# Placing the second layer's accumulations among the first layer's, and the last pairs' normalisation, in a fused attention and MLP kernel

## The chip, the cores and the metric

The kernel runs on one core of one Trainium2 chip. The metric is the device time of one execution in microseconds (us); lower is better. The engines are called TensorE (PE in the profile, its weight loads PEld), VectorE (DVE), ScalarE (ACT), GpSimd (POOL) and SyncE (SP, which here only issues transfers).

## What is computed

`x` has 2048 tokens of 640 features. It is normalised once, and the result feeds a multi-head attention with 32 heads of 20 features and a two-layer MLP (640 to 1536 to 640, GELU between) that normalises its input again. Both results are added to `x`.

```python
B, S, D, H = 1, 2048, 640, 32          # F = 1536
xn = _layernorm(x)
# attention
q, k, v = split(xn @ wqkv)             # (B, H, S, 20) each
p = softmax(einsum("bhqd,bhkd->bhqk", q, k) * 20 ** -0.5)
a = einsum("bhqk,bhkd->bhqd", p, v).reshape(B, S, D) @ wo
# MLP
h = gelu(_layernorm(xn) @ w1 + b1)
m = h @ w2 + b2
return x + a + m
```

## The kernel before

After a first part (to about 220 us) that normalises, projects q, k and v and splits the weights into pairs of 16-bit numbers, one loop (L1143) runs over 256 *groups*. The heads are taken in pairs: `ORDER` (L39) runs over pairs 0 to 11 with both halves of the queries each, then over pairs 12 to 15 with the first half of the queries, then over pairs 12 to 15 with the second half. Each such entry has eight groups: two blocks of 512 queries by four times four blocks of 128 keys.

A group issues, in this order:

- two blocks of scores (`scores`, L705: two matmuls `s` each, then ScalarE's exponential into `p`), a `tick()`, `rest` for the first block, and one portion of *fill* (`other`, L1129);
- two more blocks of scores, a `tick()`, `rest` for the others, and the products of the previous group's probabilities with v (`pv`, L730, matmuls `o`).

`rest` (L720) has VectorE compute `low`, the 16-bit remainder of two of the four probability blocks; the products need it one group later. After every fourth group `pv` has ScalarE copy its result out of PSUM (`ev`), and after eight `unload` (L771) stores it with six transfers on SP's queue.

The fill is TensorE's other work, cut into *units* by the generator `mlp` (L1015) and, after it, `projection` (L1064). `other` spreads a unit over two to four groups, so that each group gets about the same amount. The MLP goes through eight chunks of 256 tokens:

- `layer1(mc, f)` (L966) makes two of the twelve blocks of hidden features of a chunk: 30 matmuls `pu` into the one PSUM bank of pool `psM`. At its end `gelu` (L910) begins, seven operations of VectorE and one tanh of ScalarE, spread over the following ticks; the first of them (`u`, L914) sets the bank free. The result goes to `hT`, of which there are two buffers.
- `layer2(mc, j, hf)` (L998) makes 128 tokens by 320 output features from `hT`: 36 matmuls `py` into the same bank. At its end `addup` (L940) adds it onto `xb` (one operation of VectorE, L942), which sets the bank free. `xb` has one buffer: after every second such unit it is stored (L947), loaded anew with `x` (L995), and `b2` is added by a transfer on GpSimd's queue (L996).

A chunk has six first-layer units and, of the chunk before it, four second-layer units; `mlp` says in which order they stand. When a chunk's last first-layer unit is issued, the features of the chunk after the next are loaded; after the last chunk's, the output weights `wo` are loaded into the place of `w1`, and `prep_late` (L671) splits them on VectorE, eight ticks later.

The attention's results are *normalised* by their sums in `finish` (L824), for two or three pairs of heads and half of the queries at a time: sums are loaded (`lt`, L835), inverted and stored (L876 to L885), and then, for 512 queries at a time, two partial results (`oa`, L867) and the inverses (`rb`, L897) are loaded, added, multiplied and split into 16-bit numbers (L900, L902, L904, L906), and stored to `oscr` (L907). These generators are moved on by `tick` (L652), one step a tick. There are two lists: those in `sides` take a step at every tick; those in `patient` only at ticks where nothing else has just given VectorE work, or in steps that are marked as waiting. The finishes stand in one queue (`fins`) and run one after the other in one generator, `finishing`, which begins in `patient`. `unload` puts it over to `sides` under a condition (L786).

When all units of `mlp` are issued, `projection` follows: 256 tokens at a time (a *piece*), 15 matmuls `z` for each 128 tokens by 320 features, added onto the MLP's result by L1047. It needs all finishes of its half of the queries and the split of `wo`; `ahead` (L1054) loads the first piece (L1041, L1042) as soon as the first half's finishes are done. What is left of it after the last group runs at the end by itself, from about 1274 us.

Of the kernel before, what the change touches and what calls it, by code (L numbers as in the profile page):

```python
# [27 lines left out]
NPAIR = H // 2  # L28
# [9 lines left out]
TAIL = 12  # L38
# [6 lines left out]
def mha_mlp_kernel(tc, x, wqkv, wo, w1, b1, w2, b2, out):  # L45
# [4 lines left out]
    with (  # L50
# [580 lines left out]
        with ExitStack() as scope:  # L631
# [8 lines left out]
            sides, patient = [], []  # L640
# [89 lines left out]
            def pv(units):  # L730
# [29 lines left out]
                if last:  # L760
                    if cc == 0:
                        evs[g, hf] = m1.tile([P, 2, 512], F32, tag="ev", name="ev")
                    nc.scalar.activation(evs[g, hf][:, cc], pv.o, AF.Copy)  # L763
                    if cc == 1:
                        unload(g, hf, evs.pop((g, hf)))

            def dma(g, hf):

                return (nc.scalar if (g, hf) == ORDER[-1] else nc.sync).dma_start

            def unload(g, hf, ev):  # L771
                cols = slice(hf * 1024, (hf + 1) * 1024)
                direct.extend([ev] if (g, hf) == ORDER[-1] else [])
                for p in range(0 if direct else 2):
                    dma(g, hf)(lpart[p, hf, 2 * g : 2 * g + 2, :].rearrange("a (c t) -> a c t", c=2),
                                      ev[PAD + DH + VW * p :: 64])
                    for a in range(2):
                        q0, r = 64 * a + PAD + VW * p, (2 * g + a) * DH
                        dma(g, hf)(opart[p, r : r + DH, cols].rearrange("d (c t) -> d c t", c=2),
                                          ev[q0 : q0 + DH])  # L780
                if g + 1 in ENDS:
                    fins.append(finish(g + 1 - UNITS[ENDS.index(g + 1)], g + 1, hf))
                    if len(fins) == 1:
                        patient.append(finishing())
                        runner[:] = patient[-1:]
                    if hf == 1 and g + 1 > TAIL and runner[0] not in sides:  # L786

                        patient.remove(runner[0])
                        sides.append(runner[0])
# [6 lines left out]
            fins, direct, runner = [], [], []  # L796
# [22 lines left out]
            def finishing():  # L819
                while fins:  # L820
                    yield from fins[0]
                    fins.pop(0)
# [133 lines left out]
            def load_chunk(mc):  # L956
                t0 = mc * MC
                xnt = early.pop(0) if early else load_features(mc)
                r2f = m1.tile([P, MC], F32, tag="r2f", name="r2f", bufs=2)
                nc.sync.dma_start(r2f, rscr[None, t0 : t0 + MC].to_broadcast([P, MC]))  # L960
                xs[mc] = xnt, r2f
                unscaled.append(r2f)
                if mc > 1:
                    patient.append(scale_ahead(r2f))

            def layer1(mc, f):  # L966
                xnt, r2f = xs[mc]
                if f == 0:
                    hTs[mc] = m0.tile([P, KF, 2, MC], F16, tag="hT", name="hT")
                ps = psM.tile([P, 2, MC], F32, tag="m", name="pu")  # L970
                for i in range(2):
                    n = 0
                    fo_ = (f + i) % 4 * P
                    for k in range(KD):
                        for a, b in PASS:
                            nc.tensor.matmul(ps[:, i], w1v[:, k, (f + i) // 4, a, fo_ : fo_ + P], xnt[:, k, b, :],  # L976
                                             start=(n == 0), stop=(n == 3 * KD - 1))
                            n += 1
                            if n % 3 == 0:
                                if i == 1 and n == 15:  # L980
                                    begin(gelu(ps, r2f, hTs[mc], f))
                                yield 0.3276
                if f == KF - 2:
                    if mc + 2 < NMC:
                        load_chunk(mc + 2)
                    if mc + 1 == NMC:
                        sides.append(ahead())
                        sides.append(prep_late(wot, wov, wo.rearrange("(k p) n -> p k n", p=P), KD, 8))
# [9 lines left out]
            def layer2(mc, j, hf):  # L998
                t0 = mc * MC + j * P
                if t0 == 0 and hf == 0:  # L1000
                    load_xb(0)
                ps = psM.tile([P, 512], F32, tag="m", name="py")
                n = 0
                for f in range(KF):
                    for a, b in PASS:
                        nc.tensor.matmul(ps[:, :320], hTs[mc][:, f, a, j * P : (j + 1) * P],  # L1006
                                         w2v[:, f, b, hf * 320 : (hf + 1) * 320],
                                         start=(n == 0), stop=(n == 3 * KF - 1))
                        n += 1
                        if n % 2 == 0:  # L1010
                            if n == 36:
                                begin(addup(ps, xbs[t0], t0, hf))
                            yield 0.272

            def mlp():  # L1015
                load_chunk(0)
                load_chunk(1)
                yield 0.0
                for mc in range(NMC + 1):
                    first = [layer1(mc, f) for f in range(0, KF, 2)] if mc < NMC else []  # L1020
                    second = [layer2(mc - 1, j, hf) for j in range(MC // P) for hf in range(2)] if mc else []
                    done[0] = mc == NMC
                    for i in range(6):
                        if i < len(first):
                            yield 2 * KD, 3.276
                            yield from first[i]
                        if 0 < i <= len(second):
                            yield 3 * KF // 2, 4.896
                            yield from second[i - 1]

            pieces = {}

# [81 lines left out]
            def chain():  # L1114
                yield from mlp()
                yield from projection()
# [167 lines left out]
```

## Time and profile before

| | |
|---|---|
| time, median of 3 runs | 1341.68 us (1340.11 to 1343.48) |
| the profiled execution | 1341.9 us, of it 1340.0 us from the first to the last instruction |
| granted TensorE clock, mean | 0.999 |
| exponentials (L713, ScalarE) | 1024, busy 972.8 us |
| `low` (L725, VectorE) | 512, busy 614.5 us |
| `o` (L742), `s` (L711), TensorE | share of the chain of waits 28% and 18% |
| `py` (L1006), `pu` (L976), TensorE | 1152 matmuls, busy 178.5 us; 1440, busy 178.2 us |

A row of the trace in order of time begins with its start and its length in us, then engine, line, operation, `out<-in` by the program's names, shapes, and how many instructions were merged into it (x4). In square brackets is how long the engine had been idle before it and which instruction ended that. In a row of stretches, each engine's busy time is followed by its number of instructions. On the page, the line of an engine gives busy time, share of the span and number of instructions; the chain of waits is the chain that ended last, followed back from the last instruction. A line of transfers gives their size and, where it is known, the median time from issue to landing.

### The profile page before, as it was taken

The numbers are of one execution on the slowest core, as the hardware profiler recorded it, in microseconds if no ns is written. First come the engines' busy times: TensorE is split into PE (matmuls) and PEld (weight loads), VectorE is DVE, ScalarE is ACT, GpSimd is POOL, SyncE is SP. The second block draws the span as 40 slices with busy tenths as digits, with TensorE's granted clock in tenths as the row PEclk, the third lists the DMA queues.
The fourth block names the chain that finished last, engine by engine and source line by source line (L and its number), as shares of the span: only waits on it lengthen the run. The fifth ranks groups of instructions, "written<-read, shape, count | busy, mean of one in ns | idle before, by whom it ended". The sixth has DMA issues, their size and how long they took to land.

```text
span 1340.0 us, 29065 instructions
## 1 busy us (share of the span) xinstructions
PE 1328.6 (99%) x11647; PEld 588.6 (44%) x11647; DVE 1055.9 (79%) x1436; ACT 1130.1 (84%) x1306; POOL 37.5 (3%) x85
## 2 busy tenths in 40 slices
PE   9999999999999999999999999999999999999998
PEld 6645546443344433434433344334333444333366
DVE  7766945998779887978897878888887988888732
ACT  7754525999999999999999999999999999999900
POOL 3010000000000000000000000000000000000000
PEclk9999999999999999999999999999999999999999
DMA  9768731111112232122322032313032323334366
GB/s 279 253 197 183 125 128 58 34 53 43 49 52 78 87 83 73 44 69 67 91 76 71 19 103 56 88 56 94 19 83 78 85 64 103 90 113 121 104 208 187
DMA packets 100150, 129.54 MB, mean 97 GB/s; under 512 B 24276, under 2 KB 66328, under 8 KB 100012
## 3 DMA queue, kind: packets, MB, share of 16 engines
q1 hardware_dynamic: 96652, 120.25, 31.5%
q0 software_dynamic: 2912, 6.90, 2.8%
q8 instruction: 92, 1.51, 0.5%
q10 hardware_dynamic: 448, 0.51, 0.1%
q14 instruction: 46, 0.38, 0.1%
HBM read 82.14 MB, written 42.51 MB: 93 GB/s over the span
## 4 chain that ended last, share of the span: by engine, by line
PE 86%; DVE 6%; ACT 4%; issue 2%; DMA 1%; SPq 0%; ACTq 0%; DVEq 0%; POOL 0%; POOLq 0%
PE o L742 28%; PE s L711 18%; PE py L1006 13%; PE pu L976 10%; PE qkp L325 7%; PE z L1089 4%; PE vp L398 3%; DVE low L725 2%; ACT p L713 1%; PE warm L222 1%; ACT wv L431 1%; DMA oa<-opart 0%; DVE u L914 0%; ACT qkhl L340 0%; DVE u L916 0%
## 5 line engine op out<-in xcount | busy, mean ns | idle before, releaser
L713 ACT ACTIVATE p<-s 128x1024 f32<-128x1024 f32 x1024 | 972.8, 1045 | 35.0 <-PE s L711 28.6
L725 DVE TENSOR_TENSOR low<-p 128x1024 f16<-128x1024 f32 x512 | 614.5, 1219 | 144.9 <-ACT p L713 144.2
L742 PE MATMUL o<-p,vfull 128*32 128x512 bf16 (+1 forms) x4096 | 430.0, 493 | 0.0
L711 PE MATMUL s<-qs,ks 61*128 61x512 f16 x2048 | 311.9, 381 | 1.1 <-ACT p L713 1.1
L711 PEld LDWEIGHTS <-ks 61*128 61x128 f16 x2048 | 61.1, 94 | 280.1 <-issue 279.1
L1006 PE MATMUL py<-w2t,hT 128*128 128x320 f16 x1152 | 178.5, 300 | 0.5 <-DVE u L914 0.3
L976 PE MATMUL pu<-xm,w1t 128*128 128x256 f16 x1440 | 178.2, 273 | 0.0
L976 PEld LDWEIGHTS <-w1t 128*128 128x128 f16 x1440 | 131.0, 98 | 64.6 <-issue 51.0
L1006 PEld LDWEIGHTS <-hT 128*128 128x128 f16 x1152 | 102.5, 98 | 88.5 <-issue 54.1
L325 PE MATMUL qkp<-xnt,wv 128*128 128x512 f16 x600 | 131.1, 379 | 1.4 <-DVE vfull L410 0.9
L742 PEld LDWEIGHTS <-vfull 128*32 128x32 f16 x3072 | 59.8, 95 | 139.2 <-issue 108.5
L742 PE MATMUL o<-low,vfull 128*32 128x512 f16 x1024 | 102.9, 378 | 0.4 <-DVE low L725 0.2
L325 PEld LDWEIGHTS <-wv 128*128 128x128 f16 x600 | 58.1, 98 | 71.4 <-DVE vfull L410 1.2
L742 PEld LDWEIGHTS o<-p,vfull 128*32 128x32 f32 x2048 | 62.5, 108 | 52.6
L1089 PE MATMUL z<-w1t,ot 128*128 128x320 f16 x480 | 69.0, 304 | 0.4 <-DVE acc L1047 0.4
L340 ACT ACTIVATE qkhl<-qkp,qks 128x1024 f16<-128x1024 f32 (+1 forms) x24 | 23.2, 967 | 54.6 <-PE qkp L325 33.0
L398 PE MATMUL vp<-wv,xnt 128*128 128x320 f16 x480 | 66.7, 299 | 0.0
L1089 PEld LDWEIGHTS <-ot 128*128 128x128 f16 x480 | 46.7, 99 | 24.3 <-issue 5.9
L398 PEld LDWEIGHTS <-xnt 128*128 128x128 f16 x480 | 46.7, 98 | 18.4
L341 DVE SCALAR_TENSOR_TENSOR qkhl<-qkp,qks,qkhl 128x1024 f16<-128x1024 f32 (+1 forms) x24 | 26.5, 1105 | 32.6 <-ACT qkhl L340 32.5
L1047 DVE SCALAR_TENSOR_TENSOR acc<-z,sc,acc 128x320 f32<-128x320 f32 x32 | 17.4, 546 | 40.7 <-PE z L1089 40.5
L763 ACT ACTIVATE ev<-o 128x512 f32<-128x512 f32 x64 | 39.3, 614 | 2.7 <-PE o L742 2.7
(190 smaller groups left out, 672.4 us busy)
## 6 DMA issues: line engine op xcount, KB each, us to landing
qkscr<-qkhl SPq DMA_DIRECT2D x40, 256.0 KB
opart<-ev SPq DMA_DIRECT2D x124, 80.0 KB
ks<-qkscr SPq DMA_DIRECT2D x120, 80.0 KB
qs<-qkscr SPq DMA_DIRECT2D x192, 40.0 KB
oa<-opart SPq DMA_DIRECT2D x32, 240.0 KB
xt<-in_A_x_dram SPq DMA_DIRECT2D x16, 320.0 KB
xscr<-xnt SPq DMA_DIRECT2D x4, 1280.0 KB
xm<-xscr SPq DMA_DIRECT2D x8, 640.0 KB
```

What stands on the lines that cost most here:

```text
L325: nc.tensor.matmul(ps[:, i, :], wv[:, k, q, a, mm * P : (mm + 1) * P], xnts[c][:, k, b, :], start=(k + n == 0), stop=(k == KD - 1 and n == 2))
L340: nc.scalar.activation(hl[:, 0, i0:i1], ps[:, i0:i1], AF.Copy, scale=a)
L341: nc.vector.scalar_tensor_tensor(hl[:, 1, i0:i1], ps[:, i0:i1], a, hl[:, 0, i0:i1], ALU.mult, ALU.subtract)
L398: nc.tensor.matmul(ps[:, hf, :320], xnts[c][:, k, a, j * P : (j + 1) * P], wv[:, k, 2, b, hf * 320 : (hf + 1) * 320], start=(n == 0), stop ...
L711: nc.tensor.matmul(ps[:, a, :], ks[64 * a : 64 * a + 61, kb * P : (kb + 1) * P], qs[64 * a : 64 * a + 61, cc * 512 : (cc + 1) * 512], star ...
L713: nc.scalar.activation(pt, ps, AF.Exp, scale=QS)
L725: nc.vector.tensor_sub(low, pt, upper(pt))
L742: nc.tensor.matmul(pv.o[32 * q : 32 * q + 32, :], src[:, v0 - PAD * (1 - q % 2) :][:, :32], t, start=q not in pv.begun, stop=last, skip_gr ...
L763: nc.scalar.activation(evs[g, hf][:, cc], pv.o, AF.Copy)
L976: nc.tensor.matmul(ps[:, i], w1v[:, k, (f + i) // 4, a, fo_ : fo_ + P], xnt[:, k, b, :], start=(n == 0), stop=(n == 3 * KD - 1))
L1006: nc.tensor.matmul(ps[:, :320], hTs[mc][:, f, a, j * P : (j + 1) * P], w2v[:, f, b, hf * 320 : (hf + 1) * 320], start=(n == 0), stop=(n == ...
L1089: nc.tensor.matmul(ps[:, :320], ot[:, k, a, j * P : (j + 1) * P], wov[:, k, b, h * 320 : (h + 1) * 320], start=(n == 0), stop=(n == 3 * KD ...
```

## The change

In `unload`, the finishing generator is put over to `sides` not only when pairs 13 and 15 with the second half of the queries are unloaded, but also at pair 15 with the first half.

In `mlp`, the four second-layer units of a chunk no longer follow the second, third, fourth and fifth first-layer unit, but the second, third, fifth and sixth. With 0 to 5 for the first-layer units and a to d for the second-layer units of the chunk before, the order was 0 1 a 2 b 3 c 4 d 5 and is 0 1 a 2 b 3 4 c 5 d.

```diff
@@ unload
-                    if hf == 1 and g + 1 > TAIL and runner[0] not in sides:
+                    if (hf == 1 or g + 1 == NPAIR) and g + 1 > TAIL and runner[0] not in sides:
 
                         patient.remove(runner[0])
                         sides.append(runner[0])
@@ mlp
                     for i in range(6):
                         if i < len(first):
                             yield 2 * KD, 3.276
                             yield from first[i]
-                        if 0 < i <= len(second):
+                        if second and i % 3:
+
                             yield 3 * KF // 2, 4.896
-                            yield from second[i - 1]
+                            yield from second.pop(0)
```

Nothing else differs. The amount of work, the number of transfers and the sizes of all tiles are the same. After the edit in `mlp` the lines of the changed kernel are one higher.

## The prediction

> **What bounds the kernel now.** I read the engines' busy times and the chain of waits on the page first, then busy time by stretches, then TensorE's rows in order of time.
>
> ```profile
> PE 1328.6 (99%) x11647; PEld 588.6 (44%) x11647; DVE 1055.9 (79%) x1436; ACT 1130.1 (84%) x1306; POOL 37.5 (3%) x85
> PE 86%; DVE 6%; ACT 4%; issue 2%; DMA 1%; SPq 0%; ACTq 0%; DVEq 0%; POOL 0%; POOLq 0%
> 240.00:1240.00 1000.00, 998.20 (x9338) 400.53 (x9335) 852.09 (x1018) 965.87 (x1081) 13.59 (x16) 1.00 0.26 72
> 1273.70:1340.00 66.30, 59.97 (x445) 42.90 (x441) 21.14 (x41) 0.60 (x1) 0.00 (x0) 0.97 0.64 197
> ```
>
> The last two rows are stretches: length, then busy PE, PEld, DVE, ACT, POOL, clock. The change touches the first one, the attention loop. TensorE is called busy for 998 of 1000 us there, ScalarE 966, VectorE 852. Since a busy PE may hide stops, I take instead how long one turn of the loop (a "group") lasts, from the start of its run of feed-forward matmuls to the start of the next:
>
> ```profile
> 603.07 1.16 PE L976 MATMUL pu<-xm,w1t 128*128 128x256 f16 x9
> 606.89 1.48 PE L976 MATMUL pu<-xm,w1t 128*128 128x256 f16 x12
> 611.02 1.26 PE L1006 MATMUL py<-w2t,hT 128*128 128x320 f16 x8
> ...
> 619.11 1.26 PE L1006 MATMUL py<-w2t,hT 128*128 128x320 f16 x8
> ...
> 627.20 1.81 PE L976 MATMUL pu<-xm,w1t 128*128 128x256 f16 x15
> ...
> 631.66 1.81 PE L976 MATMUL pu<-xm,w1t 128*128 128x256 f16 x15
> ```
>
> A group with 9 pu lasts 3.82, with 12 pu 4.13, with 15 pu 4.46, an 8 and a 10 py together 8.09. The length follows the matmuls put in, so TensorE sets the pace, and what can be won is only what a group lasts beyond this. A chunk is 31 groups: three first-layer units as 15+15, three as 9+9+12, four second-layer units as 8+10+8+10. That is 6×4.46 + 6×3.82 + 3×4.13 + 8×8.09 = 126.8 us. The same place in seven chunks (the second group of a chunk's first second-layer unit):
>
> ```profile
> 306.79 1.53 PE L1006 MATMUL py<-w2t,hT 128*128 128x320 f16 x10
> 434.82 1.53 PE L1006 MATMUL py<-w2t,hT 128*128 128x320 f16 x10
> 561.79 1.53 PE L1006 MATMUL py<-w2t,hT 128*128 128x320 f16 x10
> 689.80 1.53 PE L1006 MATMUL py<-w2t,hT 128*128 128x320 f16 x10
> 817.20 1.53 PE L1006 MATMUL py<-w2t,hT 128*128 128x320 f16 x10
> 944.53 1.53 PE L1006 MATMUL py<-w2t,hT 128*128 128x320 f16 x10
> 1072.02 1.53 PE L1006 MATMUL py<-w2t,hT 128*128 128x320 f16 x10
> ```
>
> The cycles last 128.03, 126.97, 128.01, 127.40, 127.33 and 127.49. The second shows what a cycle can be; over it the others lose 1.06 + 1.04 + 0.43 + 0.36 + 0.52 = 3.41 us. The whole kernel holds little more than that to win.
>
> **What the first edit removes.** Now the first-layer units five, zero and one of neighbouring chunks stand next to each other. VectorE's work for such a row of three:
>
> ```profile
> 671.83 0.68 DVE L914 TENSOR_TENSOR u<-pu,r2f 128x512 f32<-128x512 f32 x1
> ...
> 673.89 1.22 DVE L725 TENSOR_TENSOR low<-p 128x1024 f16<-128x1024 f32 x1
> 675.02 0.68 DVE L920 SCALAR_TENSOR_TENSOR w<-w,u 128x512 f32<-128x512 f32 x1
> 675.63 1.22 DVE L725 TENSOR_TENSOR low<-p 128x1024 f16<-128x1024 f32 x1
> 676.76 0.68 DVE L900 TENSOR_TENSOR oa<-oa 120x512 f32<-120x512 f32 x1
> 677.36 1.22 DVE L725 TENSOR_TENSOR low<-p 128x1024 f16<-128x1024 f32 x1
> 678.50 0.69 DVE L924 SCALAR_TENSOR_TENSOR u<-w,u 128x512 f32<-128x512 f32 x1
> ...
> 680.41 1.22 DVE L725 TENSOR_TENSOR low<-p 128x1024 f16<-128x1024 f32 x1
> 680.68 1.48 PE L976 MATMUL pu<-xm,w1t 128*128 128x256 f16 x12
> ...
> 685.49 1.25 PE L1006 MATMUL py<-w2t,hT 128*128 128x320 f16 x8 [0.28 <-DVE u L914]
> ```
>
> Start to start, a low costs 1.13, the GELU's first three operations 2.06, its L920 0.61, its last three 1.91 (4.58 in all), and each operation of a normalisation 0.60 (its cast less). A group needs two lows, 2.27. I add up, group by group in the built order, VectorE's load less the group's length. In the groups of 9, 12, 8 from 676.9 the sum goes 1.35, 2.14, 3.27 us, and TensorE stops: 685.49 − 680.68 = 4.81 against 4.13, then 689.80 − 685.49 = 4.31 against 3.91, together 1.08. In the other cycles the sum reaches 3.27, 1.35, 2.43, 1.35 and 2.55, and they lose as listed; below 2 a stop is hardly to be seen, above 2.2 there is one.
>
> In the built order of the changed kernel units five and zero have a second-layer unit between them, with 16.2 us of TensorE and 0.5 of VectorE beyond the lows. Pairs are left: zero and one, three and four. The same sum gives, outside the first chunk (which has the old order in both), at most 2.50, 2.44 and 2.32 at three places (near 433, 495 and 1002 us) and 1.84 elsewhere.
>
> Not all of the 3.41 goes, because some stops are ScalarE's:
>
> ```profile
> 421.90 1.16 PE L976 MATMUL pu<-xm,w1t 128*128 128x256 f16 x9
> ...
> 423.67 0.39 PE L711 MATMUL s<-qs,ks 61*128 61x512 f16 x2 [0.29 <-ACT p L713]
> ...
> 426.17 1.48 PE L976 MATMUL pu<-xm,w1t 128*128 128x256 f16 x12
> ...
> 933.99 0.39 PE L711 MATMUL s<-qs,ks 61*128 61x512 f16 x2 [0.25 <-ACT p L713]
> ```
>
> Here a tanh and an unloading copy fall into one 9-group: 426.17 − 421.90 = 4.27, 0.45 too long; I take 0.41 for the other, scaled by the waits. In the new order both still fall so. Removed: 3.41 − 0.86 = 2.55 (between 2.0 and 3.41). Added: of the three places the first already waits for ScalarE, which lowers its sum by 0.45; the others I put at 0.3 each, 0.6 in all (0 to 1.3, by the 0.52 of the cycle that reached 2.55).
>
> **What both edits move near the end.** The normalisation of the last pairs, first half of the queries, is no longer held back: its second half moves from groups 240–242 to 235–237, with two oa loads, four rb loads and one store on SP's queue; projection piece 0's three loads follow it. The output weights' split moves with unit five from groups 236–243 to 232–239, its load equally far ahead. There VectorE's sum reaches 1.8 in groups of 12, against 1.36 before: nothing added (0 to 0.5).
>
> ```profile
> 1202.10 0.36 SPq L947 DMA_DIRECT2D accscr<-xb  x1
> 1207.69 0.85 POOL L996 DMA_DIRECT2D xb<-in_B_b_dram  x1 [39.32 <-DMA xb<-in_A_x_dram]
> xb<-in_B_b_dram POOLq DMA_DIRECT2D x16, 320.0 KB, 4.4
> 1223.51 1.14 SPq L835 DMA_DIRECT2D lt<-lpart  x2
> 1230.82 0.22 DVE L876 TENSOR_TENSOR lt<-lt 64x64 f32<-64x64 f32 x1 [2.87 <-DMA lt<-lpart]
> ```
>
> One transfer gets a new neighbour: the store L947 of the last-but-one add-up now stands behind piece 0's loads on SP. From L947 to the reloaded xb it takes 1207.69 − 1202.10 + 4.4 = 10.0 us, and the next add-up comes two pairs of 8 and 10 later, 16.2. A load issued right behind piece 0's took 7.3 (1223.51 to 1230.82); by this the 6.2 of cover shrinks to about zero. Behind a late add-up stand the next lows; but the 2.87 us that VectorE waited for lt lengthened no group. I take 0 (0 to 1).
>
> The following normalisation (pairs 12 and 13, second half of the queries) begins about one group earlier, since nothing is before it. Now it does this:
>
> ```profile
> 1247.65 1.40 PE L1089 MATMUL z<-w1t,ot 128*128 128x320 f16 x9
> ...
> 1255.33 1.40 PE L1089 MATMUL z<-w1t,ot 128*128 128x320 f16 x9
> 1256.32 0.69 DVE L900 TENSOR_TENSOR oa<-oa 80x512 f32<-80x512 f32 x1 [2.44 <-DMA oa<-opart]
> ...
> 1264.01 1.40 PE L1089 MATMUL z<-w1t,ot 128*128 128x320 f16 x9
> ```
>
> A 9-and-6 pair of z took 8.68 where the one before took 7.68: 1.00 lost to oa. Its loads stood behind six stores and three loads on SP; in the new order they stand ahead of them. I take the whole 1.00 (0 to 1.00). The last 66.3 us keep their order: nothing.
>
> **Sum.** −2.55 + 0.6 − 1.00 = −2.95 on the profiled execution's 1341.9 us; the median of the runs is 0.2 lower, so 1341.68 − 2.95 = 1338.7, put at 1338.8. With the bounds, the sum lies between −4.4 and +0.8.
>
> **The rivals.** *A, every stop goes:* with less on VectorE its L920, and so the tanh behind it, comes earlier and ScalarE's two stops go as well; the remaining 0.1 to 0.2 of each cycle over 126.8 does too: 3.41 + 1.00 + about 0.6, so 1336.7. For it: the stops come in the same groups as VectorE's sums; against it: ScalarE shows no wait for VectorE there.
>
> *B, pairs overfill VectorE as three did (slower):* seven pairs of units three and four and the split of the output weights, each now with half a normalisation in or behind it, each stopping TensorE as the 680–690 us place did: 8 × 1.08 = 8.6, less 4.4 won, 1345.9. It decides from a sum of about 1.8 on. Against it: the cycle of 126.97 has the same five-to-zero pair and a sum of 1.35.
>
> *C, ScalarE is the bound and nothing is won:* its exponentials, 966 of 1000 us busy, are untouched; stops move and stay, 1341.7. Against it: group lengths follow the matmuls. The Trainium skill (Perfetto Trace Analysis, Identifying the Most-Contended Engine) calls matmul busy time a bad measure and ranks ScalarE and VectorE by occupancy; by that rule, ScalarE leads with 97% and the time stays. The trace speaks against it here, by the 3.82 to 4.46 us of the groups.
>
> **How the numbers follow.** 0.3% is 4.0 us, about what a measurement of this kernel tells from no change: faster means below 1337.7, slower above 1345.7. The forecast gets 0.47, of which 0.14 lies below 1337.7 since its uncertainty is some 1.3 us; A 0.24, of it 0.22 faster; B 0.16, of it 0.15 slower; C 0.13. So faster 0.36, slower 0.15, same 0.49. The range takes in the forecast, A and C with half a us each side: 1336.2 to 1342.5; B's 0.16 is left out. The forecast alone lies in 1337.4 to 1340.1.
>
> **What would show it.** Right: cycles of 127 us each, no DVE u release ahead of py, the 0.3 waits of s for p near 423 and 934 still there, no DVE wait for oa near 1250. Wrong: groups over length by half a us at 495, 1002 or 1180–1205 us (B), a VectorE wait for xb near 1217, or those waits of s gone (A).

## The result and the profile after

The changed kernel takes 1337.55 us (median of 10 runs, 1335.5 to 1340.0) against 1341.93 (10 runs, 1338.66 to 1343.89) of the kernel before on the same chip: a ratio of 0.9973, 95% interval 0.9963 to 0.9983, so 2.3 to 5.0 us less. A second series gave 0.9979 (0.9957 to 1.0). The profiled execution has a span of 1338.0 us against 1340.0.

The engines' busy times on the page of the changed kernel hardly differ from those of before; its chain of waits does:

```profile
PE 1328.0 (99%) x11647; PEld 590.0 (44%) x11647; DVE 1055.1 (79%) x1436; ACT 1128.4 (84%) x1306; POOL 37.5 (3%) x85
...
PE 96%; ACT 1%; DVE 1%; issue 1%; DMA 0%; ACTq 0%; POOL 0%; DVEq 0%; POOLq 0%
```

In the chain, VectorE's share fell from 6% to 1% and ScalarE's from 4% to 1%, and TensorE's rose from 86% to 96%. Where this comes from is seen in TensorE's waits, by what ended them (total, number, longest). First the kernel before, then the changed one:

```profile
PE rb L892 <- DVE lt L883: 1.6, 1, 1.6
PE s L711 <- ACT p L713: 1.1, 4, 0.3
...
PE z L1089 <- DVE acc L1047: 0.4, 1, 0.4
PE py L1006 <- DVE u L914: 0.3, 1, 0.3
...
PE o L742 <- DVE low L725: 0.2, 1, 0.2
```
```profile
PE rb L892 <- DVE lt L883: 2.2, 1, 2.2
PE s L711 <- ACT p L713: 1.3, 4, 0.4
```

Every wait for VectorE in the loop that this view lists is gone; those for ScalarE stayed. The wait ahead of `rb` comes after the loop. TensorE's rows of the changed kernel in order of time, at the places that the prediction used:

```profile
305.54 1.53 PE L1006 MATMUL py<-w2t,hT 128*128 128x320 f16 x10
...
422.38 0.39 PE L711 MATMUL s<-qs,ks 61*128 61x512 f16 x2 [0.37 <-ACT p L713]
...
432.93 1.53 PE L1006 MATMUL py<-w2t,hT 128*128 128x320 f16 x10
...
559.81 1.53 PE L1006 MATMUL py<-w2t,hT 128*128 128x320 f16 x10
...
686.94 1.53 PE L1006 MATMUL py<-w2t,hT 128*128 128x320 f16 x10
...
803.75 0.39 PE L711 MATMUL s<-qs,ks 61*128 61x512 f16 x2 [0.19 <-ACT p L713]
...
814.31 1.53 PE L1006 MATMUL py<-w2t,hT 128*128 128x320 f16 x10
...
931.27 0.39 PE L711 MATMUL s<-qs,ks 61*128 61x512 f16 x2 [0.35 <-ACT p L713]
...
941.82 1.53 PE L1006 MATMUL py<-w2t,hT 128*128 128x320 f16 x10
...
1068.67 1.53 PE L1006 MATMUL py<-w2t,hT 128*128 128x320 f16 x10
...
1244.42 1.40 PE L1090 MATMUL z<-w1t,ot 128*128 128x320 f16 x9
...
1252.10 1.40 PE L1090 MATMUL z<-w1t,ot 128*128 128x320 f16 x9
...
1259.84 1.40 PE L1090 MATMUL z<-w1t,ot 128*128 128x320 f16 x9
```

The differences between the `py` starts are the six cycles: 127.39, 126.88, 127.13, 127.37, 127.51 and 126.85, together 763.13 against 765.23. The two pairs of `z` take 7.68 and 7.74; the 8.68 of before is gone.

Below, "six cycles" is that sum and "loop" the time from the first of these rows to the first `z` behind the last group. A "stop" is what a group lasts beyond the length that its matmuls give (3.82 with 9 `pu`, 4.13 with 12, 4.46 with 15; 3.91 with 8 `py`, 4.18 with 10). "First part" is what lies ahead of the loop's first scores, "end" what follows that first `z`.

| profiled execution | six cycles | loop | first part | end | span |
|---|---|---|---|---|---|
| before | 765.23 | 966.93 | 219.18 | 66.27 | 1339.99 |
| after | 763.13 | 964.00 | 217.94 | 68.45 | 1337.99 |
| after, second series | 763.20 | 964.06 | 223.24 | 66.12 | 1341.03 |

The loop became 2.93 us shorter, and a second execution repeats it within 0.1 us. First part and end, which the change doesn't touch, differ by 5.3 and 2.3 us between two executions of the same kernel; so one execution's span doesn't tell what the change is worth, and the experiments are read by the loop.

### The profile page after: what moved, and what is told of

It reads as the page before. It is cut to its first block, busy times and chain, and to the rows that moved or that the text cites. A ratio compares the mean times of both kernels' runs of the same rounds, so it can differ in the third digit from the quotient of the medians.

```text
span 1338.0 us, 29071 instructions
## 1 busy us (share of the span) xinstructions
PE 1328.0 (99%) x11647; PEld 590.0 (44%) x11647; DVE 1055.1 (79%) x1436; ACT 1128.4 (84%) x1306; POOL 37.5 (3%) x85
## 4 chain that ended last, share of the span: by engine, by line
PE 96%; ACT 1%; DVE 1%; issue 1%; DMA 0%; ACTq 0%; POOL 0%; DVEq 0%; POOLq 0%
PE o L742 31%; PE s L711 20%; PE py L1006 13%; PE pu L976 12%; PE qkp L325 10%; PE vp L398 5%; PE z L1090 5%; PE warm L222 1%; ACT p L713 1%; DMA lt<-ev 0%; DVE low L725 0%; PE rb L892 0%; PE norms L370 0%; ACT ev L763 0%; PE pt L287 0%
## 5 line engine op out<-in xcount | busy, mean ns | idle before, releaser
L996 POOL DMA_DIRECT2D xb<-in_B_b_dram x16 | 13.6, 849 | 986.7 <-DMA xb<-in_A_x_dram 429.8
```

## The experiments

**Each edit alone.** `order_six` is the kernel before with the new order in chunks 1 to 6 (the last chunk keeps the old one) and without the edit in `unload`; `runner_only` has the edit in `unload` alone; `after_again` is the changed kernel. All three were timed on one chip.

```diff
order_six
-                        if 0 < i <= len(second):
+                        if second and (i % 3 if mc < NMC - 1 else i):
...
-                            yield from second[i - 1]
+                            yield from second.pop(0)
runner_only
-                    if hf == 1 and g + 1 > TAIL and runner[0] not in sides:
+                    if (hf == 1 or g + 1 == NPAIR) and g + 1 > TAIL and runner[0] not in sides:
```

> The kernel before with the new order in chunks 1 to 6 alone; the last chunk's order and the list that the finishes run in are as before. Theory (the first edit takes VectorE's overload out of the six cycles, the second the wait for oa near 1250 us): the six cycles sum to 763.1 us as in the changed kernel (765.2 before), the 1.0 us at the oa wait stays, so from the start of the first cycle to the end of the loop 964.8 us (before 966.9, changed kernel 964.0). Rival (the two edits only work together): cycles near 765.2, loop 966.9. Time 0.998 of before.

> The kernel before with the second edit alone. Theory: cycles stay at 765.2 us; the wait for oa near 1250 us goes (1.0 us); the last pairs' normalisation now falls behind first-layer units, where VectorE's sum reaches 2.3 and 3.2, which costs about 0.6 us near 1145 and 1173 us; loop 966.5 us. Rival (the second edit carries the gain): loop 964. Time 1.000 of before.

> The changed kernel once more, on the same chip as its two parts. Theory: six cycles 763.1 us, loop 964.0 us, 0.997 to 0.998 of before. What differs from its first profile is then the spread of the first part (before 218 us) and of the last (from 1270 us on), where the first profile had 68.5 us against 66.3 before.

| | six cycles | loop | ratio to before, 95% |
|---|---|---|---|
| order_six | 763.18 | 964.87 | 1.0005 (0.9988 to 1.0021) |
| runner_only | 765.24 | 965.99 | 1.0012 (0.9995 to 1.0029) |
| after_again | 763.20 | 964.06 | 0.9979 (0.9957 to 1.0) |

The edits divide the gain as the theory said: the order wins 2.05 in the six cycles and nothing at the loop's end, the edit in `unload` nothing in the cycles and 0.94 at the end. The same place near 1260 us, `order_six` and then `runner_only`:

```profile
1257.74 1.40 PE L1089 MATMUL z<-w1t,ot 128*128 128x320 f16 x9
...
1260.60 0.40 PE L742 MATMUL o<-low,vfull 128*32 128x512 f16 x3 [0.15 <-DVE low L725]
...
1262.79 0.97 PE L1089 MATMUL z<-w1t,ot 128*128 128x320 f16 x6 [0.41 <-DVE acc L1047]
```
```profile
1258.14 1.40 PE L1089 MATMUL z<-w1t,ot 128*128 128x320 f16 x9
...
1262.19 0.99 PE L1089 MATMUL z<-w1t,ot 128*128 128x320 f16 x6
```

From `z` to `z` it is 5.05 where VectorE's lateness holds up `low` and then `acc`, and 4.05 without. What missed is a cost: the theory gave `runner_only` 0.6 for sums of 2.3 and 3.2 on VectorE near 1145 and 1173 us, and no group there was long; its loop is 965.99 instead of 966.5. The times of the two single edits don't show their gains of 1 to 2 us, and the 0.998 expected of `order_six` lies outside its interval. In part this goes with TensorE's granted clock, which differs between executions of one kernel (last section). Among those with a mean clock of 0.997 the kernel before takes 1345.1 us (12 executions), `order_six` 1343.0 (5), `runner_only` 1344.7 (3) and `after_again` 1342.6 (3).

**The normalisation out of VectorE's bursts.** `no_norm` is the kernel before; for pairs 0 to 11 it leaves out the sum of the two partial results and the product with the inverses, and writes copies of the inverses instead of the two halves.

```diff
+                    few = g1 <= TAIL
+                    if not few:
                         nc.vector.tensor_add(o0, o0, o1)
...
-                    nc.vector.tensor_copy(hl[:, 0], o0)
+                    nc.vector.tensor_copy(hl[:, 0], rb if few else o0)
```

> The kernel before, but for pairs 0 to 11 the finishes leave out the sum of the two partial results and the product with the inverses, and write plain copies of the inverses: 0.7 us of VectorE for each half instead of 2.1, every transfer and wait as before. Theory (VectorE's load in the row of three first-layer units makes the stops): the stops at 430, 685 and 1067 us go, those for ScalarE near 423, 804 and 934 us stay; six cycles 763.0 us. Rival (the chunk boundary itself: buffers, loads, the bank): 765.2.

The six cycles sum to 763.57, not to the 763.0 expected, since one of the three stops stayed. The third cycle fell from 128.01 to 126.94 and the first from 128.03 to 127.42; the last stayed at 127.50. TensorE's rows of `no_norm` at the places of the third and of the last:

```profile
682.87 1.49 PE L982 MATMUL pu<-xm,w1t 128*128 128x256 f16 x12
...
687.00 1.26 PE L1012 MATMUL py<-w2t,hT 128*128 128x320 f16 x8
...
690.91 1.26 PE L1012 MATMUL py<-w2t,hT 128*128 128x320 f16 x8
...
1068.83 1.25 PE L1012 MATMUL py<-w2t,hT 128*128 128x320 f16 x8
...
1071.01 0.81 PE L742 MATMUL o<-low,vfull 128*32 128x512 f16 x4
```

The groups that took 4.81 and 4.31 now take 4.13 and 3.91: these stops need the normalisation on top of the three GELUs. Near 1070 the four `o` on `low` last 0.81 instead of 0.39, and the stop is 0.55, against 0.54 before. VectorE's rows of `no_norm` ahead of it (behind its edit lines are six higher: L920 is L914 of before):

```profile
1066.56 0.55 DVE L883 RECIPROCAL lt<-lt 96x64 f32<-96x64 f32 x1
...
1068.10 0.67 DVE L920 TENSOR_TENSOR u<-pu,r2f 128x512 f32<-128x512 f32 x1
```

Here it is the inverting of the sums, which `no_norm` keeps, that stands between the GELUs; that it makes this stop is read from the rows, and no run leaves it out. So the row of three is common to the three places, and what is put into it differs.

**A row of three at another place.** `triple_moved` is the changed kernel with the units in the order 0 1 2 a 3 b 4 c 5 d: again three first-layer units side by side, but not across the border of two chunks.

```diff
-                        if second and i % 3:
+                        if second and i > 1:
```

> The changed kernel, with the four second-layer units behind the third, fourth, fifth and sixth first-layer unit (0 1 2 a 3 b 4 c 5 d): the row of three stands at the chunk's head, no unit five next to unit zero. Theory (any row of three first-layer units overfills VectorE when a normalisation falls into it): the running sum reaches 2.4 to 2.7 us in three cycles (first, third, fourth), each loses 0.3 to 0.6; six cycles 764.5 us against 763.1. Rival (only the seam between two chunks costs): 763.1 or less.

The six cycles sum to 763.64, which lies between the two. Of the three stops expected one came in full, one in small. TensorE's rows of `triple_moved` near 695 us:

```profile
694.28 1.25 PE L1006 MATMUL py<-w2t,hT 128*128 128x320 f16 x8
...
696.46 0.81 PE L742 MATMUL o<-low,vfull 128*32 128x512 f16 x4
...
698.59 0.58 PE L1006 MATMUL py<-w2t,hT 128*128 128x320 f16 x3
```

4.31 from `py` to `py` instead of 3.91, beside 0.19 in the group ahead (0.59 in all); near 440 us it was 0.16, and the third place, near 822 us, lost 0.07. A row of three can stop TensorE away from the border, but the sum of VectorE's load does not say which of them does. By itself this run decides little.

**More load on VectorE.** `heavy` is the changed kernel with one operation of the GELU done twice, 0.6 us more for every first-layer unit.

```diff
                 nc.vector.tensor_mul(w, u, u)
+                nc.vector.tensor_mul(w, u, u)
```

> The changed kernel with the GELU's square (the operation that makes w from u) done twice: 0.6 us more of VectorE for each first-layer unit, nothing else. Theory (VectorE's sum over some 2.2 us stops TensorE): at ten places of the six cycles the sum now reaches 2.4 to 3.7; six cycles 767 to 771 us against 763.1. Rival (ScalarE or TensorE alone sets the pace, VectorE is 85% busy): 763.1.

The six cycles sum to 772.24, 9.1 more than those of the changed kernel and above the 767 to 771 expected, for 36 units times 0.6 = 21.6 us of work. TensorE's rows of `heavy` near 500 us, and its waits:

```profile
500.37 1.25 PE L1007 MATMUL py<-w2t,hT 128*128 128x320 f16 x8
...
503.69 0.40 PE L742 MATMUL o<-low,vfull 128*32 128x512 f16 x3 [0.76 <-DVE low L725]
...
505.42 1.53 PE L1007 MATMUL py<-w2t,hT 128*128 128x320 f16 x10
```
```profile
PE o L742 <- DVE low L725: 7.6, 13, 0.9
```

5.05 instead of 3.91: groups of eight `py` that follow a pair of first-layer units are now too long, behind ten of the twelve pairs of the six cycles, by 0.48 to 1.14. (Three of the 13 waits lie in the first chunk, ahead of the cycles.) So the pairs of the new order, which cost 0.16 at most in the changed kernel, are for the most part less than 0.6 us a unit away from a longer stop.

**ScalarE's copies.** `ev_three` is the changed kernel, with the copy out of PSUM moved from ScalarE to VectorE for three of the 64 that the loop makes: where the copy falls into a 9-group with a tanh and TensorE then waits for `p` (near 420, 800 and 930 us).

```diff
+                    if (ORDER.index((g, hf)), cc) in ((5, 1), (17, 0), (21, 0)):
+                        nc.vector.tensor_copy(evs[g, hf][:, cc], pv.o)
+                    else:
                         nc.scalar.activation(evs[g, hf][:, cc], pv.o, AF.Copy)
```

> The changed kernel with three of the 64 copies of the products out of PSUM moved from ScalarE to VectorE: those before the stops near 420, 801 and 929 us. Theory (there ScalarE is late because a tanh and a copy fall together): these stops (0.54, 0.36 + 0.14, 0.51) go; the 0.55 us more on VectorE raise its sum to about 3.0 near 433, which gives 0.3 to 0.5 back; six cycles 762.0 us. Rival (those stops are VectorE's lateness handed on): 763.1 or more. Time as the changed kernel within its noise.

The six cycles sum to 762.11, the loop takes 962.97; ratio 0.9982 (0.9961 to 1.0004). TensorE's rows of `ev_three` at the first place and behind it, and what is left of the waits of `s`:

```profile
426.04 1.16 PE L979 MATMUL pu<-xm,w1t 128*128 128x256 f16 x9
427.12 0.66 PE L711 MATMUL s<-qs,ks 61*128 61x512 f16 x4
...
434.10 1.25 PE L1009 MATMUL py<-w2t,hT 128*128 128x320 f16 x8
...
436.28 0.81 PE L742 MATMUL o<-low,vfull 128*32 128x512 f16 x4
...
438.42 1.53 PE L1009 MATMUL py<-w2t,hT 128*128 128x320 f16 x10
```
```profile
PE s L711 <- ACT p L713: 0.3, 1, 0.3
```

The second two `s` follow the first at once (four in one row). Three stops of 0.54, 0.50 and 0.51 are gone but for a few hundredths, so they were not VectorE's lateness handed on. 0.47 comes back two groups later, at the place where the theory expected VectorE's sum to be too high: ScalarE's stop had given VectorE the time that it lacked there.

**The inverses later.** Behind the loop the last normalisation's `rb` waits for the sums, and the waiting products of the projection stand behind it on TensorE. `late_rb` is the changed kernel with ten waiting steps ahead of `rb` instead of four, so that more `z` come before it.

```diff
-                        for _ in range(4 if last else 1):
+                        for _ in range(10 if last else 1):
```

> The changed kernel with the spreading matmuls of the last inverses (rb) issued six ticks, 18 matmuls, later behind the loop. Theory (what the profiles of one kernel differ in lies in the first part and in the last; in the last, TensorE waits 1.5 to 2.5 us for the last inverses, and rb then takes 2.5 or up to 4.1 us): no wait ahead of rb, rb 2.5 us, 64 to 65 us from the end of the loop to the end against 66.1 and 68.5; 2 us faster than the changed kernel, 0.996 of before. Rival (the wait only moves to the later loads of the attention's results): 66 us or more.

The ratio is 0.9961 (0.9942 to 0.998). The changed kernel's rows, then those of `late_rb`:

```profile
1277.11 0.22 DVE L876 TENSOR_TENSOR lt<-lt 64x64 f32<-64x64 f32 x1 [2.32 <-DMA lt<-ev]
...
1278.48 4.13 PE L892 MATMUL rb<-lt,sel 64*80 64x64 f32 x32 [2.24 <-DVE lt L883]
```
```profile
1274.99 9.14 PE L1090 MATMUL z<-w1t,ot 128*128 128x320 f16 x66
1284.74 2.47 PE L892 MATMUL rb<-lt,sel 64*80 64x64 f32 x32 [0.61 <-issue]
...
1302.38 25.98 PE L1090 MATMUL z<-w1t,ot 128*128 128x320 f16 x190 [0.93 <-DMA ot<-oscr]
```

The sums come no earlier (8.0 us behind the first `z` instead of 7.6), but 66 `z` cover most of it. The loop stays at 964.05. What the rival said came in small: TensorE now waits for the later loads of the attention's results (`ot`), 0.93 us, which the changed kernel doesn't, so that its waits behind the loop are 1.54 us in all against 2.24. This alone doesn't account for an end of 64.7 instead of 68.4; the rest goes with the clock, below.

**Both together.** `both_edits` has the edits of `ev_three` and `late_rb`; `late_rb_again` ran beside it.

> The changed kernel with the ev copy on VectorE at the three groups of ev_three and ten waiting ticks ahead of rb as in late_rb. Theory (the two gains lie in different stretches and add): the six cycles sum to 762.1 us, the loop from its second py group to the first z behind it takes 963.0, the wait of TensorE ahead of rb is below 0.7 us and the tail 64 to 65 us; against the kernel before on the same chip 0.995 to 0.996. Rival (they don't add, since VectorE's later work moves the last group's end): loop 964.1 or tail above 66, ratio 0.997 or more.

> late_rb a second time, to compare with both_edits on the same chip. Theory: loop 964.05, tail 64.7, wait ahead of rb 0.6; ratio to the kernel before 0.996 to 0.997, about 1.1 us longer than both_edits. Rival (the tail of late_rb was short by the spread of executions and not by the later rb): tail 66 to 68 and rb 3 to 4 us as in the changed kernel.

| | six cycles | loop | wait ahead of rb | wait for ot | end | ratio to before, 95% |
|---|---|---|---|---|---|---|
| both_edits | 762.13 | 962.98 | 0.26 | 0.77 | 64.24 | 0.9945 (0.9926 to 0.9964) |
| late_rb_again | 763.18 | 964.02 | 0 | 0.41 | 63.54 | 0.9953 (0.9934 to 0.9971) |

The loops are as expected to 0.1 us. The ratios came out lower than expected, and their intervals overlap with each other; on this chip the medians are 1336.57 and 1338.46 against 1344.29, so `both_edits` is 7.7 us shorter than the kernel before. Its interval just touches that of the changed kernel (from 0.9963); since both were measured against the same kernel on different chips, the step from one to the other rests on the loop (−1.0) and on the end, below.

## Why the prediction was right, step by step

**TensorE sets the pace: right.** No cycle of any run is below 126.85, beside the 126.8 worked out. By the Trainium skill (Perfetto Trace Analysis, Identifying the Most-Contended Engine), which goes by the highest occupancy and sets matmul busy time aside, ScalarE would have been the bound; the prediction had this as rival C. The runs bear that out in part only: moving three copies off ScalarE won 1.0 us, but VectorE, busy 852 of 1000 us, held the greater part of what could be won, since its load came in bursts.

**"Removed: 3.41 − 0.86 = 2.55": right in kind, a little too much.** VectorE's stops of before were 0.61 near 430, 1.08 near 680 to 690 and 0.54 near 1067 us, 2.23 in all, and all are gone. The prediction also counted the 0.43 of the fourth cycle as VectorE's. This one is ScalarE's: near 800 us the stop is 0.49 before and 0.50 after (the fourth cycle lasts 127.40 and 127.37) and goes only when its copy moves (126.89 in `ev_three`). The kernel before had this wait for ScalarE, too:

```profile
806.64 0.39 PE L711 MATMUL s<-qs,ks 61*128 61x512 f16 x2 [0.20 <-ACT p L713]
```

Three of the stops belong to ScalarE, not two. Three stops of less than 0.1 (near 546, 673 and 1056 us, 0.23 together) went as well, so that 2.46 was removed.

**"Added 0.6 (0 to 1.3)": right in size by chance.** At the places named, 495 and 1002 us, the groups have their length; 0.46 came instead, as 0.15 or 0.16 each near 626, 880 and 1134 us, where the prediction put the sum at 1.84 or less:

```profile
626.04 1.26 PE L1006 MATMUL py<-w2t,hT 128*128 128x320 f16 x8
...
630.10 1.53 PE L1006 MATMUL py<-w2t,hT 128*128 128x320 f16 x10
```

That is 4.06 instead of 3.91. The limit of 2.2 on the sum of VectorE's load is what failed: sums put at 2.44 and 2.32 stopped nothing here, nor did the 2.3 and 3.2 of `runner_only`. It had been read in part from the fourth cycle (2.43), whose stop is ScalarE's. That ScalarE's stop covers the place near 433 was right: `ev_three` took it away and got 0.47.

**ScalarE's stops near 423 and 934 stay: right.** Together with the beginnings of them in the group ahead they were 0.52 and 0.49 and are 0.54 and 0.51.

**The oa wait, −1.00: right.** VectorE's wait of 2.44 us for `oa` is gone. From the first `z` to the end of the loop the changed kernel takes 0.94 less; `runner_only` shows the same 0.94 and `order_six` none of it.

**At nothing: right.** VectorE has no wait for `xb`, and TensorE none in the groups with the output weights' split.

**The sum, −2.95.** The loop shows −2.93. In the prediction's terms it is −2.46 + 0.46 − 0.94 = −2.94 instead of −2.55 + 0.6 − 1.00: three errors of up to 0.14 that cancel, which is luck. The median lies 1.2 us under the forecast, which the interval of 2.3 to 5.0 us less allows for; first part and end differ by more than that from one execution to the next.

**The rivals.** A fell by the waits of `s` that stayed. B's mechanism is real, as `heavy` shows, and its places are where the added 0.46 came: these three groups stand behind a pair of units three and four with half a normalisation in it. But they cost 0.15 or 0.16 each, not the 1.08 of a row of three, and the other four pairs of these units at most 0.02. One GELU operation more in each unit would have brought the full price. C fell as a whole, though 1.5 us of it are there.

Open is why VectorE's sum stops TensorE at one place and not at another with the same sum. At the three small stops, and at none of the other four pairs, the normalisation's first two operations (L900, L902) stand between those of unit four's GELU (L900 at 621.73, 876.22 and 1130.59 us). The sum has no place for how far ahead a `low` is of the product that needs it; no run varied this alone.

## What to carry to other kernels

Where a loop's turns follow one engine's work, measure each turn against what its own instructions give, and look at the few that are longer; an engine that is busy 85% on average can still stop the others wherever its bursts meet. Spread such bursts before taking work away, and find out for each stop by itself which engine causes it, since a stop of one engine can cover that of another. Compare a stretch that the change touches and that repeats, not the whole span, when the gain is a few tenths of a per cent.

## What the runs showed of the hardware

The end varies with TensorE's granted clock. Stretches from the first `rb` on (columns as in the prediction: length, busy PE, PEld, DVE, ACT, POOL, clock, share of transfers, GB/s) of the changed kernel, of the kernel before and of `order_six`:

```profile
1278.40:1282.60 4.20, 4.12 (x33) 4.03 (x34) 0.35 (x1) 0.00 (x0) 0.00 (x0) 0.56 0.80 243
1279.00:1285.00 6.00, 6.00 (x38) 4.85 (x37) 0.00 (x0) 0.00 (x0) 0.00 (x0) 0.50 0.87 254
```
```profile
1282.00:1284.50 2.50, 2.49 (x33) 2.43 (x34) 0.28 (x1) 0.00 (x0) 0.00 (x0) 1.00 0.68 226
1285.00:1288.00 3.00, 3.00 (x13) 1.67 (x12) 0.00 (x0) 0.00 (x0) 0.00 (x0) 0.50 0.70 203
```
```profile
1283.00:1291.00 8.00, 6.73 (x64) 5.51 (x65) 3.48 (x9) 0.00 (x0) 0.00 (x0) 1.00 0.84 246
```

The same 32 `rb` take 4.13 us at a mean clock of 0.56 and 2.47 at 1.00. Taken microsecond by microsecond, the clock here is 1.00 or 0.50, but for those in which it changes, and it stays at 0.50 for 3.4 or for 6.8 us. Over all twelve profiled executions:

| clock behind the wait ahead of rb | executions | wait | rb | end |
|---|---|---|---|---|
| 0.50 for 6.8 us, beginning within rb | after, ev_three, runner_only, no_norm | 1.62 to 2.46 | 3.08 to 4.13 | 67.8 to 68.7 |
| 0.50 for 3.4 us, beginning behind rb | before, after_again, heavy | 1.45 to 1.73 | 2.47 | 66.1 to 66.4 |
| stays at 1.00 | order_six, triple_moved | 1.44 to 1.46 | 2.47 | 64.4 to 64.5 |
| stays at 1.00 | late_rb, late_rb_again, both_edits | 0 to 0.61 | 2.47 to 2.50 | 63.5 to 64.7 |

Half the clock for 3.4 us is 1.7 us less of TensorE's work, for 6.8 us 3.4 us less (an estimate from these lengths); the ends of the first two rows lie 1.6 to 2.0 and 3.3 to 4.3 us above that of the third. The last two rows end nearly alike, since the runs with a later `rb` wait 0.41 to 0.93 us for `ot` instead. So what `late_rb` wins is in the main the clock, and the timed executions agree: of the 23 with a later `rb` none had a mean clock below 0.998, of the 31 of the kernel before on the same two chips 13 had.

A wait of 1.4 us or more ahead of `rb` was followed by a lower clock in seven of nine executions, waits of at most 0.93 behind the loop in none of three. That the wait brings the lower clock about is likely, but a wait alone doesn't decide it. In the first part TensorE waits 1.9 to 2.3 us for VectorE near 122 us in nine of the twelve executions; the clock then fell to 0.50 for 3.4 us in four of them (`after_again`, `order_six`, `ev_three`, `late_rb`) and not in the other five. This is also what the first part's spread goes with: it takes 217.9 to 220.1 us in the three executions where TensorE waits at most 1.24 us there, 221.0 to 222.0 with the longer wait alone, and 223.2 to 223.7 with the longer wait and the lower clock. In the loop the clock was 1.00 in all twelve. No run varied a wait by itself with all else unchanged.
